# One gate and up tile moved from the attention's filler to the seven-product phase, in a block of sliding attention and a gated layer

## The chip, the core and the metric

The kernel runs on one NeuronCore of a Trainium2 chip, as one program. The metric is the device time of one execution in microseconds (us), given as the median of several runs.

The engines are called by the names of the profile: PE is TensorE's matmul, PEld its weight load, DVE is VectorE, ACT is ScalarE, POOL is GpSimd, and SP is SyncE, whose queue issues nearly all transfers here. L111 is line 111 of the kernel's file.

## The reference

Cut to what is computed (S = 2048 rows, D = 640 columns, 32 heads of 20, a window of 256 rows, a hidden width of 1728):

```python
xn = _layernorm(x)
q, k, v = (xn @ wqkv) split into 3 x 32 heads of 20
scores = q @ k.T * 20 ** -0.5        # only where 0 <= i - j < 256
o = softmax(scores) @ v
att = o.reshape(S, D) @ wo
h = gelu(xn @ w_gate) * (xn @ w_up)
out = x + att + h @ w_down
```

All tensors are float32.

## The kernel before

**Products.** A float32 factor is split in two parts, high and low, each of a type that TensorE takes at one pass. A plain product of two split factors is three products: high by high, low by high and high by low. With D = 640 in five slices of 128 rows, one group of 128 outputs by a chunk of 512 rows takes 3 x 5 = 15 TensorE products of 512 columns (`dense_steps`, L111). The 2048 rows are four chunks of 512.

**Stages.** The program has four stages on TensorE: the layer norm with the first projections; the attention; the phase of the gate and up products; and the phase of the last products (w_down and wo together, L1237).

**The attention.** It goes through 32 units, four chunks for each of eight groups of four heads. A unit has NS = 14 slots, and the code writes out by hand, slot by slot, what each engine gets to do. In a unit lie: the maxima (`max_pair`, L525 on PE and L529 on DVE, two pairs at slots 0, 4 and 8, and two more behind the output products), the scores with their exponential (`exp_piece`, L584 and L586, at slots 2, 4, 6, 8 and 10), the masks on POOL (`clear`, L597 and L600), and the output products of the unit before at slot 0 (`av_unit`, L624), whose sum POOL makes (L630). At slot 9 the k rows of a later unit are loaded and at slot 12 its q rows (`load_stack`, L496). The maxima of that later unit begin at slot 4 of the next unit. There are three q tiles, so a q load waits until the scores of the running unit have read the old one. The scores, maxima and output products use a ring of six PSUM banks; the filler has two banks of its own.

**The filler.** At the end of each slot TensorE gets products that have nothing to do with the unit, so that it has work while the other engines deal with the scores: `pull_fill(RATE / NS)`. A product of 512 columns counts 1.0 and one of 320 columns 0.65. Ahead of the first unit 12 portions of 8 and two of 8 are handed out. The generator `filler` gives them in this order: the last chunk of the first q and k tiles; then the list `sets`. A set ("qk", i) is the q tile i and the k tile i + 5, four chunks each, 120 products; a set ("gu", f) is the gate and the up tile f, four chunks each, 120 products too. At the place V1_AT the second half of V is projected (16 x 15 products of 320 columns); the first half's last rows come within the first set. The last set of the list, the half tile f = 13, is only split here and multiplied right behind the attention.

A projected q or k group goes on as follows (`save_qk`): ACT copies it to bf16 (L278), DVE subtracts (L274, into the single tile r), ACT copies again (L259), POOL subtracts (L260), and SP stores it to DRAM (L269), from where `load_stack` takes it. A gate and up group goes through ACT and DVE (L673 to L694) and is stored as h. Weights are loaded into the two buffers of `wrp` and split by ACT and POOL (L655, L660) while the set before runs; the split halves alternate between two pools, `pools[(s + 1) % 2]`.

**The phase of the gate and up products.** Tiles f = NFA to 12 are multiplied there by a scheme with seven products in place of eight (`gate_up_pair`, L970): for each tile and each of the two pairs of chunks, sums of the weights (`w_sums`) and of the rows (`x_sums`, made by POOL during the attention) take part, and there are 54 TensorE products of 512 columns, 108 for a tile, where the plain way has 120. A tile there has in addition its sums on DVE and its copies on ACT, and between them run jobs for the last phase (`work`).

```python
def pull_fill(n):
    debt[0] += n
    while debt[0] > 0:
        debt[0] -= next(fill, 1.0)
```

Of the kernel before, what the change touches and what calls it, by code (L numbers as in the profile page):

```python
# [25 lines left out]
NF = 14  # L26
# [5 lines left out]
NS = 14  # L32
BURSTS = 0, 4, 8
SCORES = {2: range(0, 3), 4: range(3, 5), 6: range(5, 7), 8: range(7, 9), 10: range(9, 12)}
RATE = 34.05
V1_AT = "gu", 0, 3
VEARLY = 2
VLEAD = 40
POOL_SLOTS = 13, 0, 1, 2, 3, 4, 5, 6, 7
MXD = 6  # L40
KSLOT = 9
LAG = 3, 5, 4, 4, 4, 4, 3, 3, 4, 3, 2, 1, 1, 1
NFA = 4
HD = D // 2
HR = 5
NQD = 9
# [25 lines left out]
def block_kernel(ctx, tc, x, wqk, wv, wgu, wdo, wdl, out):  # L72
# [414 lines left out]
    def load_stack(u, which=(0, 1)):  # L487
        g, c = divmod(u, NC)
        for m in range(80 * g // 128, (80 * g + 79) // 128 + 1):
            assert all((m + 5 * i, c) in done for i in which), (u, m)  # L490

        for i in which:
            dst, src, top, again = ((qs[u % NQ], qd[c], 1, 2), (ks[u % NK], kd[c], 0, 0))[i]
            for j in (0, 2):
                for p, part, n in ((j * 32, top, 2), (j * 32 + 2 * DH, again, 1), (64 - j * 32, 0, 3)):
                    nc.sync.dma_start(dst[p:p + DH * n, j:j + 2].rearrange("p j t -> p (j t)"),  # L496
                                      src[g, part:part + n].rearrange("s (d j) t -> (s d) (j t)",
                                                                      j=4)[:, j * C:(j + 2) * C])
# [140 lines left out]
    def load_gu(f):  # L639
        raws = []  # L640
        for i in range(2 if f < NF - 1 else 1):
            raw = wrp.tile([128, KT, 128], F32, name="wr", tag="wr")
            nc.sync.dma_start(raw, wgu[2 * f + i])
            raws.append(raw)
        return raws
# [4 lines left out]
    def split_later(pool, bufs, raw):  # L650
        hi = pool.tile([128, KT, 128], F32R, name="wqh", tag="wqh", bufs=bufs)
        lo = pool.tile([128, KT, 128], F32R, name="wql", tag="wql", bufs=bufs)

        def high():
            nc.scalar.activation(hi, raw, AF.Copy)  # L655
            for k in range(KT):
                defer(1 + k, when_free, low, k)

        def low(k):
            nc.gpsimd.tensor_tensor(out=lo[:, k], in0=raw[:, k], in1=hi[:, k].bitcast(F32), op=OP.subtract)  # L660

        defer(1, high)
        return hi, lo
# [37 lines left out]
                                   lambda k: xh[:, k, cs], lambda k: xl[:, k, cs], KT)  # L701
            defer(1, *((late, c4) if i else (c1,)))

    sets = [("qk", 1), ("qk", 2), ("qk", 3), ("gu", 0), ("qk", 4)]
    sets += [("gu", f) for f in range(1, NFA)] + [("gu", NF - 1)]
    pools = (wp, None), (hp, 2)
    rest = []

    def filler():
# [6 lines left out]
        for s, (kind, i) in enumerate(sets[:-1]):  # L716
            nxt = []
            after = sets[s + 1]
            for c in range(NC):
# [14 lines left out]
                if c in (1, 2) and c <= len(raws):  # L734
                    nxt.append(split_later(*pools[(s + 1) % 2], raws[c - 1]))
                if pending and (kind, i, c) == V1_AT:
                    pending = False
# [79 lines left out]
# [5 lines that stand above are left out]
    def attention():  # L822
# [18 lines left out]
        for u in range(NU + 1):  # L841
            for i in range(NS):
# [14 lines left out]
                if u + 3 < NU and i in (KSLOT, 12):  # L857
                    load_stack(u + 3, (int(i == KSLOT),))
                pull_fill(RATE / NS)
        while acts or idle:  # L860
# [458 lines left out]
    order.__enter__()  # L1319
    raws_w = load_gu(NFA)  # L1320
    banks = [psg.tile([128, C], F32, name="ps_g", tag=f"g{i}") for i in range(4)]
# [32 lines left out]

    raws_next = {NFA + 1: load_gu(NFA + 1)}
    for j, f in enumerate(range(NFA, NF - 1)):
        end = f + 1 == NF - 1
# [92 lines left out]
    for n, (p, k) in enumerate(steps):  # L1450
        i = n % (NQD + 1)
# [74 lines left out]
```

## Time and profile before

| | |
|---|---|
| median of 3 runs | 1032.83 us (1032.82, 1032.83, 1249.1) |
| the execution that was profiled | 1033.91 us |
| its span, first to last instruction | 1032.2 us |
| granted TensorE clock, mean | 0.999 |
| TensorE busy | 1020.8 us, 10941 products |
| moved from and to memory | 158.95 MB |

The page of a profile describes one execution. Its span is the time from the first to the last instruction; busy times are sums over an engine's instructions, and instructions on TensorE overlap, so the distance from one start to the next is what a product costs there. A row of the timeline gives the start, the length, the engine, the line and the tiles (written <- read), and in brackets the idle time of the engine ahead of it with what ended it. In the timeline and in the list of windows all times are counted from the span's start.

### The profile page before, as it was taken

The numbers are of one execution on the slowest core, as the hardware profiler recorded it, in microseconds if no ns is written. First come the engines' busy times: TensorE is split into PE (matmuls) and PEld (weight loads), VectorE is DVE, ScalarE is ACT, GpSimd is POOL, SyncE is SP. The second block draws the span as 40 slices with busy tenths as digits, with TensorE's granted clock in tenths as the row PEclk, the third lists the DMA queues.
The fourth block names the chain that finished last, engine by engine and source line by source line (L and its number), as shares of the span: only waits on it lengthen the run. The fifth ranks groups of instructions, "written<-read, shape, count | busy, mean of one in ns | idle before, by whom it ended". The sixth has DMA issues, their size and how long they took to land.

```text
span 1032.2 us, 28689 instructions
## 1 busy us (share of the span) xinstructions
PE 1020.8 (99%) x10941; PEld 853.4 (83%) x10941; DVE 710.5 (69%) x2007; ACT 528.3 (51%) x1120; POOL 380.0 (37%) x543
## 2 busy tenths in 40 slices
PE   8999999999999999999999999999999999999998
PEld 8987676777788877777777888888888999999998
DVE  8844655666665566676644778776556879888887
ACT  4444667766676666766666423222224544333332
POOL 5232777877665578667664111110110000000000
PEclk9999999999999999999999999999999999999999
DMA  5642464655432364534324557767127864434342
GB/s 203 191 143 70 136 198 138 179 160 178 123 106 86 96 177 135 158 121 133 121 67 134 178 200 244 249 230 245 67 79 259 263 215 146 138 124 131 111 133 93
DMA packets 105203, 158.95 MB, mean 154 GB/s; under 512 B 15420, under 2 KB 60092, under 8 KB 105064
## 3 DMA queue, kind: packets, MB, share of 16 engines
q1 hardware_dynamic: 102680, 150.95, 46.0%
q10 hardware_dynamic: 2384, 6.16, 1.9%
q8 instruction: 86, 1.41, 0.6%
q14 instruction: 53, 0.43, 0.1%
HBM read 101.78 MB, written 54.92 MB: 152 GB/s over the span
## 4 chain that ended last, share of the span: by engine, by line
PE 85%; DMA 4%; DVE 4%; POOL 2%; ACT 1%; issue 1%; SPq 1%; DVEq 0%; ACTq 0%; POOLq 0%
PE ps_g L970 20%; PE ps_d L111 20%; PE ps L1237 18%; PE ps_e L584 7%; PE ps_v L111 7%; PE ps_o L624 6%; PE ps_m L525 4%; PE ps_g L111 1%; DMA qs<-qd 1%; PE ps_t L182 1%; POOL pt L260 1%; DVE at L1075 1%; DMA kd<-pt 1%; DVE wb L1075 1%; DMA hd<-hr 1%
## 5 line engine op out<-in xcount | busy, mean ns | idle before, releaser
L529 DVE CUSTOM_DVE_ANT_0 junk<-ps_m,mask 128x288 bf16<-128x288 f32 (+2 forms) x512 | 197.6, 441 | 127.0 <-PE ps_m L525 126.1
L586 ACT ACTIVATE P<-ps_e 128x512 f32<-128x512 f32 (+2 forms) x384 | 195.4, 574 | 54.8 <-PE ps_e L584 53.6
L1237 PE MATMUL ps<-wb,at 128*128 128x320 f32 x999 | 156.4, 309 | 0.8 <-DVE xr L1263 0.8
L1237 PEld LDWEIGHTS ps<-wb,at 128*128 128x128 f32 x999 | 148.9, 188 | 1.6 <-issue 1.0
L597 POOL TENSOR_SCALAR_AFFINE_SELECT P<-P 128x512 f32<-128x512 f32 x128 | 84.5, 661 | 86.2 <-ACT P L586 80.6
L584 PE MATMUL ps_e<-qs,ks 124*128 124x128 bf16 (+2 forms) x704 | 107.2, 277 | 1.6 <-DVE mx L529 1.3
L111 PE MATMUL ps_d<-xh,wqh 128*128 128x512 f32 x350 | 105.2, 410 | 0.0
L111 PE MATMUL ps_d<-xh,wql 128*128 128x512 f32 x350 | 105.1, 410 | 0.0
L111 PE MATMUL ps_d<-xl,wqh 128*128 128x512 f32 x350 | 105.1, 409 | 0.0
L1237 PE MATMUL ps<-wt,at 128*128 128x320 f32 x552 | 89.3, 309 | 0.4 <-DVE u L1075 0.4
L584 PEld LDWEIGHTS <-ks 124*128 124x128 bf16 x704 | 51.6, 98 | 40.7 <-issue 24.2
L1237 PEld LDWEIGHTS ps<-wt,at 128*128 128x128 f32 x552 | 82.9, 188 | 0.9 <-DVE u L1075 0.9
L1191 ACT ACTIVATE at<-ss 128x512 fp32r<-128x512 f32 x59 | 37.3, 632 | 89.9 <-DVE ss L1075 89.9
L104 POOL TENSOR_TENSOR wql<-wr,wqh 128x640 fp32r<-128x640 f32 x11 | 17.7, 1609 | 173.1 <-PE ps_g L970 129.3
L600 POOL TENSOR_SCALAR_AFFINE_SELECT P<-P 128x512 f32<-128x512 f32 x112 | 72.0, 653 | 16.5 <-ACT P L586 16.4
L624 PE MATMUL ps_o<-P,v 64*32 64x320 f32 (+5 forms) x2816 | 77.1, 347 | 0.2 <-POOL P L600 0.2
L111 PEld LDWEIGHTS ps_d<-xh,wql 128*128 128x128 f32 x350 | 63.9, 189 | 13.0 <-issue 2.1
L111 PEld LDWEIGHTS ps_d<-xh,wqh 128*128 128x128 f32 x350 | 63.2, 189 | 13.2 <-issue 2.6
L111 PEld LDWEIGHTS ps_d<-xl,wqh 128*128 128x128 f32 x350 | 63.6, 189 | 12.5 <-issue 2.3
L624 PEld LDWEIGHTS ps_o<-P,v 64*32 64x32 f32 x2816 | 66.9, 106 | 4.8 <-POOL P L600 1.4
L260 POOL TENSOR_TENSOR pt<-r,pt 128x512 bf16<-128x512 f32 x40 | 46.9, 1173 | 56.6 <-ACT pt L259 56.3
L525 PE MATMUL ps_m<-ks,qs 60*32 60x96 bf16 (+4 forms) x3008 | 61.0, 244 | 1.8 <-DMA qs<-qd 1.4
(196 smaller groups left out, 1906.9 us busy)
## 6 DMA issues: line engine op xcount, KB each, us to landing
hr<-hd SPq DMA_DIRECT2D x104, 128.0 KB
hd<-he SPq DMA_DIRECT2D x50, 256.0 KB
wr<-wgu SPq DMA_DIRECT2D x27, 320.0 KB
qs<-qd SPq DMA_DIRECT2D x64, 120.0 KB
ks<-kd SPq DMA_DIRECT2D x64, 120.0 KB
xi<-x SPq DMA_DIRECT2D x16, 320.0 KB
qs<-qd SPq DMA_DIRECT2D x64, 80.0 KB
ks<-kd SPq DMA_DIRECT2D x64, 80.0 KB
```

The lines of the kernel that those rows point to most:

```text
L111: nc.tensor.matmul(ps, a(k), b(k), start=n == 0, stop=n == 3 * nk - 1)
L260: nc.gpsimd.tensor_tensor(out=pt[:, l, :], in0=r, in1=pt[:, 1, :], op=OP.subtract)
L525: nc.tensor.matmul(ps[32 * h:32 * h + 32, lo:hi], q[rows, j, q0:q0 + 32], keys, start=True, stop=True, tile_position=(64 * r, 32 * h))
L529: nc.vector.tensor_tensor_reduce(out=junk[:, 0:n], in0=ps[:, 0:n], in1=mask[:, 288 - n:288], scale=1.0, scalar=NEG, op0=OP.add, op1=OP.max ...
L584: nc.tensor.matmul(ps[:, col:col + n], k[0:QROWS, j, kc:kc + 128], q[0:QROWS, j, q0:q0 + n], start=True, stop=True)
L586: nc.scalar.activation(pt[:, j, lo:hi], ps[:, lo:hi], AF.Exp, scale=SCALE)
L597: nc.gpsimd.affine_select(out=a, in_=a, pattern=[[0, 4], [1, 128]], compare_op=OP.is_ge, fill=0.0, base=0, channel_multiplier=-1)
L600: nc.gpsimd.affine_select(out=a, in_=a, pattern=[[0, 4], [-1, 128]], compare_op=OP.is_ge, fill=0.0, base=-1, channel_multiplier=1)
L624: nc.tensor.matmul(halves[h][32 * j:32 * j + 32, q0:q0 + n], v[rows, w0_:w0_ + 32], pts[u, bi][rows, j, col:col + n], start=i == 0, stop=i ...
L970: nc.tensor.matmul(ps, i, j, start=first and n == 0, stop=n == len(work) - 1, skip_group_check=True)
L1191: nc.scalar.activation(hi[:, 3:7], s, AF.Copy)
L1237: nc.tensor.matmul(ps[bank][:, 0:HD], *work[bank][j], start=bank not in begun, stop=final[p, bank] == n and j == len(work[bank]) - 1, skip ...
```

## The change

Tile f = 3 leaves the filler and is multiplied in the phase behind the attention, which then has the tiles 3 to 12. The four q and k sets follow each other without the tile f = 0 between the third and the fourth. V's second half, which stood behind tile 0, now stands within the last q and k set, behind its chunk 1. The rate of the filler goes from 34.05 to 30.4 per unit.

```diff
-RATE = 34.05
-V1_AT = "gu", 0, 3
+RATE = 30.4
+V1_AT = "qk", 4, 1
...
-NFA = 4
+NFA = 3
...
-    sets = [("qk", 1), ("qk", 2), ("qk", 3), ("gu", 0), ("qk", 4)]
-    sets += [("gu", f) for f in range(1, NFA)] + [("gu", NF - 1)]
+    sets = [("qk", i) for i in range(1, 5)] + [("gu", f) for f in range(NFA)] + [("gu", NF - 1)]
```

Three places in the order of the instructions show what moves. (One line fewer stands ahead of the attention's end in the new file, so its later lines are one lower.)

The first is SP's queue in the fourth unit of the attention, around the q load of chunk 2 for the second group of heads (qs is the q tile, ks the k tile; qd and kd are the stored q and k rows in DRAM, pt the tile they are stored from, wr and wvr raw weights). Before:

```order
L496 DMA ks_171<-kd_90 60x1024
L269 DMA qd_84<-pt 64x3x512 x2
L238 DMA wr<-wqk 128x640 x2
L496 DMA qs_166<-qd_86 40x1024
L496 DMA qs_166<-qd_86 20x1024
```

Now:

```order
L496 DMA ks_171<-kd_90 60x1024
L295 DMA wvr<-wv 128x320 x2
L496 DMA qs_166<-qd_86 40x1024
L496 DMA qs_166<-qd_86 20x1024
L496 DMA qs_166<-qd_86 60x1024
L496 DMA qs_166<-qd_86 40x1024
L496 DMA qs_166<-qd_86 20x1024
L496 DMA qs_166<-qd_86 60x1024
L269 DMA qd_84<-pt 64x3x512 x2
L238 DMA wr<-wqk 128x640 x2
```

The store of the projected q rows and the two weight loads have moved from ahead of the q load to behind it; V's raw weights stand ahead of it now. In the units behind this one the new queue repeats itself: q load, q store, the stores of the unit's output, k store, k load.

The second place is on TensorE, the end of the last unit: the last scores (ps_e), the filler (ps_d) and the beginning of the last output products (ps_o). Before:

```order
L584 MATMUL ps_e<-qs_167,ks_172 128x384
L111 MATMUL ps_d<-xh_79,wqh 128x512 x2
L111 MATMUL ps_d<-xh_79,wql 128x512 x5
L111 MATMUL ps_d<-xl_83,wqh 128x512 x3
L624 MATMUL ps_o<-P,v 32x320 x8
```

Now:

```order
L584 MATMUL ps_e<-qs_167,ks_172 128x384
L111 MATMUL ps_d<-xh_79,wql 128x512 x3
L111 MATMUL ps_d<-xl_83,wqh 128x512 x5
L624 MATMUL ps_o<-P,v 32x320 x8
```

Ten filler products stand between the last scores and the last output products before, eight now. Behind the output products came two more of the filler before; now the filler is used up there and the half tile 13 (ps_g) follows at once.

The third is on ScalarE, where V's second half begins (L332 saves a V group, L673 and L683 belong to a gate and up group, L278 and L259 to a q or k group). Before:

```order
L673 ACTIVATE gs<-ps_d 128x512
L674 ACTIVATE he<-ps_d 128x512
L628 ACTIVATE ob<-ps_o 128x512
L629 ACTIVATE P<-ps_o 128x512
L586 ACTIVATE P<-ps_e 128x512 x5
L683 ACTIVATE he<-he 128x512
```

Now:

```order
L278 ACTIVATE pt<-ps_d 128x512
L655 ACTIVATE wqh<-wr 128x640
L586 ACTIVATE P<-ps_e 128x512 x5
L259 ACTIVATE pt<-r 128x512
L332 ACTIVATE v<-ps_v 128x4x20 x4
```

The last group ahead of V was a gate and up group of tile 0 and is now a k group of the fourth set.

## The prediction, made before the changed kernel ran

> **What bounds the kernel now.** I read the page's busy times first, then the attention and the phases behind it as stretches, then the chain that ended last, TensorE's waits, and at last single stretches of the timeline.
>
> ```profile
> span 1032.2 us, 28689 instructions
> PE 1020.8 (99%) x10941; PEld 853.4 (83%) x10941; DVE 710.5 (69%) x2007; ACT 528.3 (51%) x1120; POOL 380.0 (37%) x543
> ...
> core 0: us, PE busy (x) PEld busy (x) DVE busy (x) ACT busy (x) POOL busy (x), PEclk, DMA share, GB/s
> 104.80:552.10 447.30, 443.93 (x7307) 331.97 (x7308) 271.61 (x1075) 302.14 (x655) 314.14 (x461) 1.00 0.46 136
> 555.30:568.90 13.60, 13.60 (x61) 11.22 (x61) 11.63 (x17) 8.31 (x13) 2.72 (x2) 1.00 0.58 176
> 568.90:788.90 220.00, 220.00 (x973) 182.13 (x972) 155.09 (x259) 69.93 (x131) 23.90 (x16) 1.00 0.55 189
> ...
> 104.80:162.50 57.70, 56.53 (x907) 41.08 (x908) 34.64 (x141) 40.50 (x82) 41.72 (x60) 1.00 0.53 157
> 162.50:220.50 58.00, 56.04 (x945) 40.12 (x944) 36.09 (x145) 39.63 (x81) 50.39 (x73) 1.00 0.57 167
> 220.50:281.70 61.20, 61.07 (x1011) 44.55 (x1014) 37.97 (x149) 41.33 (x84) 43.03 (x64) 1.00 0.50 154
> ```
>
> The span is 1032.2 us; the execution that was profiled took 1033.91 us, so 1.7 us lie around the span, and the median of the runs shown is 1032.83 us. TensorE is busy 99%. The first long stretch runs from the first unit's output products to the last unit's, 31 units of attention: 447.30/31 = 14.43 us a unit, with 447.30 - 443.93 = 3.37 us of TensorE idle. Of these, 1.17 and 1.96 us lie in the first eight units (the two rows from 104.80 and 162.50). The seven-product phase (568.90 to 788.90) has no idle at all. The granted clock is 1.00 everywhere. So what is to be priced is TensorE's instructions, and then the few places where it waits.
>
> ```profile
> 555.28 13.64 PE ps_g L111 x60
> 568.92 208.09 PE ps_g L970 x918
> ...
> L970 PE MATMUL ps_g<-xh,wqh x162: 389/389/389, 568.8 to 788.4; 128*128 128x512 f32 x162
> ```
>
> The chain gives the price: 60 plain products of 512 columns follow each other in 13.64 us, 0.2273 us each, and 918 of the seven-product phase in 208.09 us, 0.2267 us each. (The 389 ns of the last row is the length of one instruction; they overlap, and only the distance counts.) A tile of the phase has 54 such products for each of its two pairs of chunks, 108, of which 18 are of the row's kind: 162/18 = 9 tiles, f = 4 to 12.
>
> **The change part by part.** (1) Tile f = 3 leaves the filler: 2 weights x 4 chunks x 15 = 120 products, 120 x 0.2273 = 27.28 us of TensorE less in the attention. RATE goes along: it hands out 30.4 instead of 34.05 products in each of 32 units, 3.65 x 32 = 117 less. (2) The tile joins the phase: 108 x 0.2267 = 24.48 us more, as TensorE there never waits and the phase has done nine such tiles at this pace. The tile brings 23 VectorE, 14 ScalarE and 2 GpSimd instructions; those of the nine tiles keep these engines busy 155.09, 69.93 and 23.90 of 220 us and hide under the products. If that cover were gone, VectorE's share, 155/9 = 17 us, would show; at 70% busy it isn't. The sum of both is -2.80 us.
>
> (3) Every filler segment gets shorter, by 3.65/14 = 0.26 product or 0.059 us a slot. What waits under the filler gets less cover: mainly the load of the next q tile on SP's queue, which may begin when the last scores (slot 10) have read the old tile and must have landed at the maxima of slot 4 of the next unit. Eight filler segments lie between, so the cover shrinks by 8 x 0.059 = 0.47 us.
>
> ```profile
> 145.04 1.33 SPq L269 DMA_DIRECT2D qd<-pt  x2
> 146.41 1.12 SPq L238 DMA_DIRECT2D wr<-wqk  x2
> 147.63 2.28 SPq L496 DMA_DIRECT2D qs<-qd  x6
> 153.90 0.19 PE L525 MATMUL ps_m<-ks,qs 60*32 60x32 bf16 x1 [0.49 <-DMA qs<-qd]
> 154.74 0.52 PE L525 MATMUL ps_m<-ks,qs 60*32 60x32 bf16 x31 [0.65 <-DMA qs<-qd]
> ...
> 179.74 3.36 SPq L496 DMA_DIRECT2D qs<-qd  x6
> 185.00 0.38 PE L525 MATMUL ps_m<-ks,qs 60*32 60x32 bf16 x28
> ...
> 307.24 2.15 SPq L496 DMA_DIRECT2D qs<-qd  x6
> 315.74 0.46 PE L525 MATMUL ps_m<-ks,qs 60*32 60x32 bf16 x32
> ```
>
> The profile has no landing times, but three loads bound them. At 185.00 the maxima start without a wait 1.90 us behind the end of the issue (179.74 + 3.36), so a load can land in 1.90 us. At 307 there are 6.35 us, far more than needed; this is the stage of V's products. At 153.90 and 154.74 TensorE waits, 3.99 and 4.83 us behind the issue's end: the issue was late because a store of projected q rows and two weight loads stood ahead of it (145.04 to 147.53), and the transfers were crowded. So the cost of (3) lies between nothing (1.90 us suffices) and 0.47 us in each unit that also projects q and k. In the new order of SP's queue 15 q loads have a q store behind them, which marks these units: 15 x 0.47 = 7.1 us.
>
> The Trainium skill, page "DMA: Bandwidth & Descriptors", section "Anatomy of one DMA — SWDGE (gpsimd) path", gives about 2.0 us as the fixed part of one transfer on GpSimd's path. By that figure (an estimate, as these loads go by SP's queue) a q load would fit everywhere but where it is issued late, and (3) would cost nothing; the first of the loads above agrees, the one at 147.63 took twice that.
>
> (4) The order of the sets and the new rate change what stands ahead of those loads. Each unit now gives out 30.4 products, that is one q and one k product group of 15 each, so one store of each kind per unit, always at the same slots; before it was 34.05/15 = 2.27, drifting through the unit. The new queue of SP shows it: the q store stands behind the q load in each of these units, and none stands ahead. What that may save is bounded by the idle of the attention: 0 to 3.37 us. The second wait of that stage has the same root:
>
> ```profile
> 173.37 1.17 POOL L260 TENSOR_TENSOR pt<-r,pt 128x512 bf16<-128x512 f32 x1
> 174.57 0.69 DVE L274 TENSOR_TENSOR r<-ps_d,pt 128x512 f32<-128x512 f32 x1 [4.09 <-POOL pt L260]
> 175.69 1.13 PE L584 MATMUL ps_e<-qs,ks 124*128 124x128 bf16 x6 [1.34 <-DVE mx L529]
> ```
>
> Two groups were projected so close together that VectorE stood 4.09 us for the single tile r until GpSimd had done with the one before, the maxima behind it came late, and TensorE waited 1.34 us for a bank. With 2.03 groups a unit instead of 2.27 this comes less often. Of the 2.48 us in these two places I take 1.2 as saved, and 0.8 as lost by (3), where the rows lean to its lower end (1.90 us is enough): -0.4 us together.
>
> (5) V's second half: a product of 512 columns counts 1 in the filler, one of 320 columns 0.65. Ahead of it stood 30 (chunk 3 of the first pair) + 58.5 (the rest of V's first half) + 3 x 120 (q and k sets) + 120 (tile 0) = 568.5, of which 12 x 8 + 16 = 112 are handed out before the first unit: it begins 456.5/34.05 = 13.4 units into the attention. Now it is 30 + 58.5 + 360 + 60 = 508.5, and (508.5 - 112)/30.4 = 13.0 units; its 16 x 15 x 0.65 = 156 end at 18.0 and 18.2. The last rows are needed by unit 19, whose output products stand at the head of unit 20: 1.8 units, some 25 us, to spare. Cost nothing.
>
> (6) The end of the attention: 8 filler products instead of 10 stand between the last scores and the last output products, and the 2 behind them are gone.
>
> ```profile
> 551.32 0.84 PE L111 MATMUL ps_d<-xl,wqh 128*128 128x512 f32 x3
> 552.09 2.54 PE L624 MATMUL ps_o<-P,v 64*32 64x320 f32 x96
> 552.71 0.64 POOL L597 TENSOR_SCALAR_AFFINE_SELECT P<-P 128x512 f32<-128x512 f32 x1
> ```
>
> The last mask ends at 553.35; the products that read it are the last third of the 2.54 us, from 553.8. They come 2 x 0.227 = 0.45 us earlier, just the slack; 0 to 0.2 us, taken as nothing.
>
> Sum: 24.48 - 27.28 - 0.4 = -3.2 us. The profiled execution would go from 1033.91 to 1030.7 us, and the median from 1032.83 to **1029.6 us**.
>
> **The rivals.** *The loads decide* (slower): in the new beat the store of k rows stands straight ahead of the k load, and the q load behind that, in each unit. If GpSimd is late with its part of the k rows, all three are late each time, and TensorE waits at slot 4. It decides from the point where a load's cover, 1.90 us at the tightest, is gone; its price is (3)'s upper end, 7.1 - 2.8 = +4.3 us, 1037.1 us. For it: GpSimd's 50.39 of 58.00 us in the stretch from 162.50. Against it: fewer groups per unit, so less for GpSimd.
>
> *All idle of the attention goes* with the regular beat: -2.8 - 3.37, 1026.7 us. For it, 3.13 of the 3.37 us lie where groups were projected; against it, less cover.
>
> *The attention does not shrink*, as something else paces it: the 27.28 us turn into waits and the phase still costs 24.48: 1057.3 us. Against it: 0.8% idle of TensorE, and GpSimd, the busiest of the others, would have about 50 us for four units of 54.7 us (58.0 - 4 x 0.83). The Trainium skill, "Perfetto Trace Analysis", section "Identifying the Most-Contended Engine", says that matmul busy time is no good measure and weight-load busy is better: 331.97 of 447.30 us here is 74%, against 83% in the phase. By that rule the attention has room on TensorE and this case could be true; the waits that the trace shows there speak against it.
>
> *The change doesn't do what it says*, the tenth tile costing as much as it saves (120 products): 0 instead of -2.8, 1032.4 us with the -0.4. Against it: the count of products in the code.
>
> **How the numbers follow.** The forecast has 0.60 (1028.3 to 1031.5), the loads 0.18 (1031.5 to 1037.1), all idle gone 0.16 (1026.7 to 1028.3), no shrinking 0.03, nothing gained 0.03. The range from 1026.7 to 1037.1 takes in the bounds of (3) and (4) and leaves out only the case of no shrinking. A measurement of this kernel can tell 2%, some 20 us, from no change; only the case of no shrinking passes that, so slower has 0.03, faster 0.01 and same 0.96.
>
> **What would show it.** The chain should hold 108 more products of the phase and the phase should be 244.5 us long; a unit of attention should last (14.43 - 0.83) = 13.6 us, the first output products of the last unit coming some 26 us earlier. TensorE's idle between the first and the last unit's output products should be 2 to 4 us. I am wrong if that idle is above 6 us, if the phase has waits, or if a unit stays above 14 us.

## The result: 1048.68 us, 1.4% slower, and the profile after

The changed kernel takes 1048.68 us (median of 5 runs, 1046.04 to 1049.54) against 1032.83 us before, a ratio of 1.014 with a 95% interval of 1.0128 to 1.0152. The ratio comes from the single runs, without the one of 1249.1 us before, which lies far above all others; the two medians by themselves give 1.0153. The execution that was profiled took 1048.68 us, 14.8 more than the one of before. The forecast was 1029.6 us, at most 1037.1. By the 2% of the prediction this is still "same", to which it gave 0.96, but the interval is narrow enough to tell 1.4% from nothing.

The first lines of the page after, and the two rows of its chain that stand for the half tile 13 and the seven-product phase (start, length, engine, tile, line, count):

```profile
span 1047.0 us, 28712 instructions
...
PE 1023.6 (98%) x10929; PEld 851.1 (81%) x10929; DVE 717.2 (69%) x2018; ACT 524.6 (50%) x1120; POOL 373.2 (36%) x535
```

```profile
545.75 13.82 PE ps_g L111 x60
559.57 244.80 PE ps_g L969 x1080
```

TensorE has 12 products fewer than before, as counted, and is busy 2.8 us longer in a span that is 14.8 us longer. The phase is as forecast: ten tiles in one unbroken piece of 244.80 us. So the time is lost ahead of it. The output products of the attention mark its length (line 624: shortest, median and longest duration in ns, then the first and the last start). Before:

```profile
L624 PE MATMUL ps_o<-P,v x2816: 214/376/504, 103.7 to 554.4; 64*32 64x320 f32 x67, 64*32 64x64 f32 x32, 64*32 64x256 f32 x29, 64*32 64x128 f32 x29
```

After:

```profile
L624 PE MATMUL ps_o<-P,v x2816: 214/376/504, 102.9 to 545.5; 64*32 64x320 f32 x67, 64*32 64x64 f32 x35, 64*32 64x192 f32 x30, 64*32 64x256 f32 x26
```

450.7 us have become 442.6, 8.1 less, where 26 were forecast; the phase begins at 559.57 instead of 568.92, 9.35 earlier, while 27.28 us of work are gone. Some 18 us are lost in the attention. Where, the list of stretches shows (columns as in the prediction). The first stretch, 104 to 300 us, holds most of the q and k groups, before also tile 0; it is the q and k stage. The second, 300 to 520, holds V's second half (289 to 355 us after), the last q and k groups (to 388 us after, to 415 before) and the gate and up tiles. Before:

```profile
104.00:300.00 196.00, 192.59 (x3225) 140.88 (x3209) 122.57 (x492) 132.30 (x273) 149.21 (x224) 1.00 0.52 155
300.00:520.00 220.00, 219.89 (x3703) 167.36 (x3701) 138.48 (x554) 146.89 (x338) 146.26 (x212) 1.00 0.43 127
```

After:

```profile
104.00:200.00 96.00, 89.27 (x1507) 63.52 (x1507) 56.57 (x230) 62.70 (x127) 73.67 (x107) 0.98 0.50 143
200.00:300.00 100.00, 95.16 (x1663) 70.74 (x1663) 60.97 (x252) 65.94 (x147) 76.98 (x118) 1.00 0.57 167
...
104.00:300.00 196.00, 184.43 (x3169) 134.26 (x3170) 117.54 (x481) 128.64 (x273) 150.65 (x224) 0.99 0.53 156
300.00:520.00 220.00, 217.39 (x3795) 161.51 (x3801) 138.50 (x567) 144.62 (x332) 140.94 (x209) 1.00 0.40 120
...
390.00:520.00 130.00, 127.78 (x2219) 90.61 (x2226) 86.61 (x341) 82.85 (x167) 84.20 (x127) 1.00 0.42 127
```

TensorE's idle goes from 3.41 to 11.57 us in the first stretch and from 0.11 to 2.61 us in the second, 10.7 us more together; of the 2.61 us, 2.22 lie behind 390 us, where only gate and up tiles are left (the last row). This part is the gate and up stage; where an expectation below gives a number for that stage, it means the whole second stretch. A clock of 0.98 in the first 96 us adds some 0.02 x 96 = 1.9 us. The remainder of the 18, some 5 us, is in no row. A part of it can hide in the stops themselves: a product of 512 columns has a length of 0.389 us, while the next could start after 0.227, so up to 0.16 us of a stop behind it counts as busy. I have not counted this stop by stop, and it is not shown.

What TensorE waits for in the whole run after (total us, times, longest):

```profile
PE ps_m L525 <- DMA qs<-qd: 8.1, 8, 1.6
...
PE ps_e L584 <- DVE mx L529: 1.3, 8, 0.2
PE ps_o L624 <- POOL P L600: 1.3, 1, 1.3
```

The first of these was 1.4 us, 3 times, before. The same list for SP's queue between 104 and 300 us has the stores' wait for GpSimd's part of a projected group, after:

```profile
SPq L269 <- POOL pt L260: 32.9, 11, 4.8
```

And before:

```profile
SPq L269 <- POOL pt L260: 18.9, 8, 3.7
```

How the one makes the other is seen in a unit of this stage, here from 203 us on (timeline of SP's queue, of GpSimd and of TensorE after):

```profile
205.56 1.26 SPq L269 DMA_DIRECT2D kd<-pt  x2
206.88 0.60 SPq L295 DMA_DIRECT2D wvr<-wv  x1
207.59 3.49 SPq L496 DMA_DIRECT2D ks<-kd  x6
211.18 0.35 SPq L760 DMA_DIRECT2D td<-tx  x1
211.64 2.17 SPq L496 DMA_DIRECT2D qs<-qd  x6
...
203.18 1.22 POOL L600 TENSOR_SCALAR_AFFINE_SELECT P<-P 128x512 f32<-128x512 f32 x2
204.37 1.16 POOL L260 TENSOR_TENSOR pt<-r,pt 128x512 bf16<-128x512 f32 x1
...
215.19 0.17 PE L525 MATMUL ps_m<-ks,qs 60*32 60x32 bf16 x1 [0.19 <-issue]
216.16 0.45 PE L525 MATMUL ps_m<-ks,qs 60*32 60x32 bf16 x31 [0.81 <-DMA qs<-qd]
```

GpSimd gets to the k group (L260) only behind its masks (L600) and ends at 205.53. The store of that group is at the head of SP's queue, and starts at 205.56. The k load, which has nothing to do with this store, is issued behind it, the q load behind that; its issue ends at 213.81, and at 216.16, 2.35 us later, TensorE has waited 0.81 us. This order, k store, k load, q load, comes back in each of the 13 units that fall into this stage. Their q loads start 2.1 to 5.3 us behind the end of the last scores that read the old tile, and in eight of the 13 TensorE then waits for them.

In the gate and up stage there is no q or k group. There the waits are for VectorE, mostly for its maxima, where the end of a gate and up group (L687, L694) follows the end of a unit's maxima (VectorE's timeline after, then TensorE's):

```profile
437.45 0.72 DVE L538 TENSOR_SCALAR nm<-mx 128x16 bf16<-128x16 f32 x1
438.20 0.66 DVE L539 SCALAR_TENSOR_TENSOR nm<-mx,nm 128x16 bf16<-128x16 f32 x1
438.78 0.68 DVE L687 TENSOR_TENSOR gs<-ps_d,gs 128x512 f32<-128x512 f32 x1
439.56 0.69 DVE L694 SCALAR_TENSOR_TENSOR he<-he,gs 128x512 f32<-128x512 f32 x1
...
440.68 0.22 PE L546 MATMUL ps_n<-identb,nm 128*128 128x128 bf16 x1 [0.30 <-DVE mx L529]
```

VectorE gets to the next maxima (L529) only at 440.17, behind these four, and TensorE stands until 440.68. That the four are the cause is read from the rows.

The theory: **the place of the beat decides**. 30.4 products in a unit are two groups of 15, so whatever a group does on ACT, DVE, POOL and SP comes at nearly the same slots in each unit (the 0.4 left over moves it only slowly); at the place where it lies now it is in the way, each time. The rivals: the order of the sets, the load slots, or GpSimd's load as such. That SP's queue is the path from the place to the loss, and not something else that GpSimd does late, is a question of its own, which the later experiments take up.

### The profile page after: what moved, and what is told of

It is laid out like the page before. It is cut to its first block, busy times and chain, and to the rows that moved or that the text cites. A ratio compares the mean times of both kernels' runs of the same rounds, so it can differ in the third digit from the quotient of the medians.

```text
span 1047.0 us, 28712 instructions
## 1 busy us (share of the span) xinstructions
PE 1023.6 (98%) x10929; PEld 851.1 (81%) x10929; DVE 717.2 (69%) x2018; ACT 524.6 (50%) x1120; POOL 373.2 (36%) x535
## 4 chain that ended last, share of the span: by engine, by line
PE 64%; DVE 4%; DMA 2%; issue 1%; POOL 1%; ACT 1%; SPq 0%; DVEq 0%; POOLq 0%
PE ps_g L969 23%; PE ps L1236 19%; PE ps_d L111 6%; PE ps_e L584 4%; PE ps_o L624 4%; PE ps_v L111 3%; PE ps_m L525 2%; PE ps_g L111 1%; DMA hr<-hd 1%; DVE junk L529 1%; DMA stg<-wtd 1%; DVE nm L538 0%; ACT P L586 0%; DVE ss L1074 0%; DVE at L1074 0%
## 5 line engine op out<-in xcount | busy, mean ns | idle before, releaser
L529 DVE CUSTOM_DVE_ANT_0 junk<-ps_m,mask 128x288 bf16<-128x288 f32 (+2 forms) x512 | 197.7, 442 | 156.4 <-PE ps_m L525 155.6
L597 POOL TENSOR_SCALAR_AFFINE_SELECT P<-P 128x512 f32<-128x512 f32 x128 | 84.1, 659 | 86.2 <-ACT P L586 79.6
L111 PE MATMUL ps_d<-xh,wqh 128*128 128x512 f32 x310 | 98.2, 420 | 0.0
L111 PE MATMUL ps_d<-xl,wqh 128*128 128x512 f32 x310 | 95.1, 412 | 0.0
L111 PE MATMUL ps_d<-xh,wql 128*128 128x512 f32 x310 | 91.3, 408 | 0.0
L600 POOL TENSOR_SCALAR_AFFINE_SELECT P<-P 128x512 f32<-128x512 f32 x112 | 70.3, 638 | 13.7 <-ACT P L586 13.7
L111 PEld LDWEIGHTS ps_d<-xl,wqh 128*128 128x128 f32 x310 | 55.9, 190 | 14.6 <-issue 5.8
L525 PEld LDWEIGHTS <-qs 60*32 60x32 bf16 x3008 | 32.8, 90 | 42.8 <-issue 30.1
L260 POOL TENSOR_TENSOR pt<-r,pt 128x512 bf16<-128x512 f32 x40 | 46.9, 1172 | 53.3 <-ACT pt L259 53.3
L111 PEld LDWEIGHTS ps_d<-xh,wql 128*128 128x128 f32 x310 | 56.6, 189 | 10.6 <-issue 0.5
```

Of the source, the lines that this page charges most:

```text
L111: nc.tensor.matmul(ps, a(k), b(k), start=n == 0, stop=n == 3 * nk - 1)
L260: nc.gpsimd.tensor_tensor(out=pt[:, l, :], in0=r, in1=pt[:, 1, :], op=OP.subtract)
L525: nc.tensor.matmul(ps[32 * h:32 * h + 32, lo:hi], q[rows, j, q0:q0 + 32], keys, start=True, stop=True, tile_position=(64 * r, 32 * h))
L529: nc.vector.tensor_tensor_reduce(out=junk[:, 0:n], in0=ps[:, 0:n], in1=mask[:, 288 - n:288], scale=1.0, scalar=NEG, op0=OP.add, op1=OP.max ...
L597: nc.gpsimd.affine_select(out=a, in_=a, pattern=[[0, 4], [1, 128]], compare_op=OP.is_ge, fill=0.0, base=0, channel_multiplier=-1)
L600: nc.gpsimd.affine_select(out=a, in_=a, pattern=[[0, 4], [-1, 128]], compare_op=OP.is_ge, fill=0.0, base=-1, channel_multiplier=1)
```

## The experiments

Each time is the median; the time of the kernel before, measured alongside, stands beside it. Two experiments first split the change: the new order of the sets with the old count of tiles and the old rate, and the old order with the new ones.

**The order alone.** The kernel before with

```
-V1_AT = "gu", 0, 3
+V1_AT = "qk", 4, 2
...
+    sets = [("qk", i) for i in range(1, 5)] + [("gu", f) for f in range(NFA)] + [("gu", NF - 1)]
```

> The kernel before, with the new order of the sets alone (four q and k sets in a row, V's second half within the fourth, behind chunk 2); four tiles in the filler and the rate 34.05 as before. Theory A, the beat: waits come from the rate, which at 30.4 gives one q and one k group per unit at fixed slots, so that a late store of k rows stands ahead of every load; at 34.05 the groups drift. Then 1031 to 1035 us and 3 to 6 us of idle of TensorE in the attention. Theory B, the order: waits come from q and k sets that follow each other without a pause; then 1040 us or more, with waits for q loads in the units 4 to 17.

Measured: 1033.15 us, before 1032.66; ratio 0.9995 (0.9982 to 1.0008). At the old rate the order costs nothing.

**The rate alone.** The changed kernel with the sets as before (tile 0 between the third and the fourth q and k set) and V1_AT = "gu", 0, 2; the rate 30.4 and NFA = 3 stay.

> The changed kernel with the old order of the sets (tile 0 between the third and the fourth q and k set, V's second half behind its chunk 2); three tiles in the filler and the rate 30.4 as changed. Theory A, the beat: 1043 to 1050 us, the waits for q loads up to about 170 us as in the changed kernel, and those behind about 350 us too. Theory B, the order: 1029 to 1034 us.

Measured: 1045.17 us, before 1032.66; ratio 1.0123 (1.0098 to 1.0148). The loss comes with the rate of 30.4 and the three tiles, which go together, not with the order.

**The store later.** If the store's wait holds SP's queue, issue it when its data is there:

```
-            defer(2, store)
+            defer(7, store)
```

> The changed kernel with the stores of projected q and k rows issued seven slots behind the last GpSimd step in place of two, so that in each unit they stand behind both loads in SP's queue. If the queue's order makes the q loads late, TensorE's waits for them (8 to 12 us in the changed kernel's trace between 100 and 300 us) go, and the time is 1037 to 1041 us. If the load on GpSimd or the transfers themselves make them late, it stays at 1046 to 1050 us.

Measured: 1049.87 us, before 1032.66; ratio 1.0165 (1.0135 to 1.0195). No gain; the time lies where the rival was expected. Yet the waits for q loads are gone from TensorE's list, but ACT now waits for the tile pt (three buffers) that the late store holds, and TensorE for ACT (ACT's waits in this run, then TensorE's):

```profile
ACT pt L278 <- DMA kd<-pt: 10.0, 8, 2.2
```

```profile
PE ps_m L525 <- ACT P L586: 4.0, 5, 1.7
```

So the queue's order does make the q loads late: with the store behind them they are on time. But one wait was traded for another, and this run didn't tell how much of the lost time comes by the queue.

**The maxima later.**

```
-MXD = 6
+MXD = 7
```

> The changed kernel with the product that turns the maxima (max_end) one slot later, 7 in place of 6. If the waits of 0.4 to 1.2 us per unit behind 350 us come from that product, which stands in TensorE's queue ahead of maxima that VectorE has not finished, they go: 4 to 6 us less, 1042 to 1045 us. If VectorE is late as such, the wait only moves to the next scores, and the time stays within 1.5 us of 1048.7.

Measured: 1045.46 us (1043.94 to 1052.31), before 1032.66; ratio 1.013 (1.0094 to 1.0166). By its interval this is not told apart from the changed kernel. Its trace, of the slowest of these runs, has TensorE busy 218.84 of the 220 us of the second stretch (217.39 after), and 181.41 of 196 in the first (184.43 after).

**The beat moved.** GAP is the portion of the filler ahead of the first unit; less of it puts every later group later in its unit, by 8 products or 3.7 slots. The products stay the same; the eight that are not handed out there come at the filler's end.

```
-GAP = 16
+GAP = 8
```

> The changed kernel with 8 in place of 16 filler products ahead of the first unit, so that the beat of one q and one k group per unit comes some four slots later: k stores at slots 12 and 11 in place of 9 and 8, q stores at 5 to 1 in place of 0. Theory A1, the place of the beat: the time depends on where the groups fall; here the k load stands ahead of the k store, the q load still behind it: some of the waits go, 1038 to 1046 us. Theory A2, less cover: every slot has 0.06 us less filler, wherever the groups fall: 1046 to 1050 us with about the same idle of TensorE.

Measured: 1031.81 us, before 1033.34; ratio 0.9992 (0.9976 to 1.0008). All of the loss is gone, more than either theory expected. Its two stretches:

```profile
104.00:300.00 196.00, 192.53 (x3346) 140.79 (x3345) 120.82 (x502) 137.19 (x294) 156.61 (x233) 1.00 0.57 162
300.00:520.00 220.00, 219.24 (x3753) 163.64 (x3751) 141.19 (x553) 150.76 (x336) 147.68 (x214) 1.00 0.40 119
```

Its output products, and its phase in the chain:

```profile
L624 PE MATMUL ps_o<-P,v x2816: 214/376/505, 100.9 to 528.0; 64*32 64x320 f32 x66, 64*32 64x64 f32 x32, 64*32 64x192 f32 x29, 64*32 64x128 f32 x29
```

```profile
543.66 244.85 PE ps_g L969 x1080
```

TensorE's wait for q tiles, and SP's for GpSimd between 104 and 300 us:

```profile
PE ps_m L525 <- DMA qs<-qd: 3.4, 5, 1.0
```

```profile
SPq L269 <- POOL pt L260: 12.3, 14, 1.6
```

And the k load, the k store and the q load in the timeline of SP's queue, at the place shown of after:

```profile
209.53 2.23 SPq L496 DMA_DIRECT2D ks<-kd  x6
...
212.76 1.31 SPq L269 DMA_DIRECT2D kd<-pt  x3
214.17 3.03 SPq L496 DMA_DIRECT2D qs<-qd  x6
```

The k load now stands ahead of the k store, and SP waits less for the store: 12.3 us in place of 32.9. The first stretch is as full as before the change (192.53 and 192.59 us), the second nearly so. The last output products start 554.4 - 528.0 = 26.4 us earlier than before, as the forecast had it (some 26), and the phase begins 568.92 - 543.66 = 25.3 us earlier.

The other direction, about 3 slots earlier:

```
-GAP = 16
+GAP = 22
```

> The changed kernel with 22 filler products ahead of the first unit, so that the beat comes some three slots earlier: k stores at slots 5 and 2, well ahead of the k load at 9, q stores at 12 and 11, ahead of the q load. Theory A1, the place of the beat: another time than with 16 or 8, by 4 us or more, either way. Theory A2, less cover: 1046 to 1050 us again.

Measured: 1034.71 us, before 1033.34; ratio 1.002 (1.0005 to 1.0034), with TensorE busy 192.94 of 196 and 220.00 of 220 us. It is 14 us from the time at 16, as theory A1 asks, but only 3 from that at 8. So it isn't "later is better", but the place at 16 that is bad.

**The k load a slot earlier.**

```
-KSLOT = 9
+KSLOT = 8
```

> The changed kernel with the k load emitted at slot 8 in place of 9. In the units 1 to 5 it then stands ahead of the k store (slot 9), in later units (k store at slot 8) still behind. If the k store in front makes the loads late, TensorE's waits for q loads go in the trace up to about 180 us and stay behind that: 3 to 5 us less, 1043 to 1046 us. If not, 1047 to 1050 us.

Measured: 1042.88 us, before 1033.34; ratio 1.0098 (1.0083 to 1.0113). A part of the loss is gone, and the run has its own control. In the early units the k load now precedes the store (SP's queue from 140 us on), in the later ones, whose store moves up as well, it doesn't (from 200 us on):

```profile
140.84 4.24 SPq L496 DMA_DIRECT2D ks<-kd  x6
145.18 1.33 SPq L269 DMA_DIRECT2D kd<-pt  x3
...
147.57 2.19 SPq L496 DMA_DIRECT2D qs<-qd  x6
...
200.45 1.25 SPq L269 DMA_DIRECT2D kd<-pt  x2
201.82 2.69 SPq L496 DMA_DIRECT2D ks<-kd  x6
...
205.53 3.36 SPq L496 DMA_DIRECT2D qs<-qd  x6
```

From the end of a q load's issue to its first maxima there are 2.5 to 3.4 us in units 5 to 8 (0.8 to 2.6 after), and 0.3 to 1.1 us, no better than after, in units 9 to 11. TensorE's waits for q tiles go accordingly: up to 181 us from 4.4 us after to none here, behind that only from 3.7 to 2.9.

**GpSimd freed in the q and k stage.** The sums for the phase (`x_sums`) move out of it:

```
-XS0, XSN = 24, 50
+XS0, XSN = 196, 28
...
-                at(XS0 + XSN * i + 5 * j, when_free, fn)
+                at(XS0 + XSN * i + 27 * j // 10, when_free, fn)
```

> The changed kernel with the 80 sums of the rows on GpSimd (x_sums) moved out of the stage of the q and k groups: from slots 24 to 419 to slots 196 to 416, in closer steps. GpSimd then has about 2 us less per unit of 14 us up to slot 190. If GpSimd's lateness with the k rows is what makes the loads late, the waits between 100 and 290 us go from 13.9 us in the changed kernel to below 6 and the time to 1037 to 1041 us, unless the later stage pays. If GpSimd is not the cause, they stay above 10 us.

Measured: 1043.7 us, before 1033.34; ratio 1.0104 (1.0088 to 1.0119). GpSimd is busy 19.5 us less than after between 104 and 300 us, yet two thirds of the loss stay; the idle between 104 and 300 us, 6.6 us, lies between what the two theories expected. Its stretches:

```profile
104.00:200.00 96.00, 89.97 (x1547) 64.21 (x1548) 55.00 (x238) 63.77 (x129) 62.78 (x92) 1.00 0.50 144
200.00:300.00 100.00, 99.41 (x1711) 74.04 (x1709) 60.74 (x261) 70.03 (x162) 68.36 (x105) 1.00 0.52 153
300.00:520.00 220.00, 216.17 (x3752) 159.15 (x3750) 141.14 (x561) 142.89 (x321) 164.06 (x240) 1.00 0.43 127
```

Behind 200 us it helps as much as it can, ahead of it hardly at all (89.97 against 89.27), though GpSimd has 10.9 us less to do there; and the stage that has the sums now is slower for it. GpSimd's load has a share in the loss; it isn't the whole of it. SP's wait for L260 between 104 and 300 us is even longer here than after, 36.3 us against 32.9, while TensorE's for q tiles falls from 8.1 to 4.3 us: how long SP stands doesn't say what it costs.

**Is there a better place?** GAP = 6, GAP = 10, and GAP = 8 together with MXD = 7:

> Changed kernel with GAP 16 -> 6, the beat one or two slots later than with GAP 8. If the place of the beat decides and there is a broad good stretch around GAP 8, 1030 to 1033 us; if GAP 8 was a narrow lucky place, 1036 us or more. Best case by the base sum (24.48 - 27.28 against the kernel before's 1033): about 1030.

> Changed kernel with GAP 16 -> 10, the beat between GAP 8 (1031.8) and GAP 16 (1048.7). If the place of the beat decides by the margin of the loads, between the two but nearer to GAP 8, 1032 to 1040 us; a smooth fall of the loss with the distance from GAP 16. If the two runs differ for another reason, no order in it.

> Changed kernel with GAP 16 -> 8 and MXD 6 -> 7. MXD 7 took some 2 us of the waits for the maxima in the gate and up stage at GAP 16; at GAP 8 that stage has almost no waits left (219.24 of 220 us busy), so by the theory of the beat it gains nothing here: 1031 to 1033 us. If MXD 7 were a gain of its own, 1029 to 1030.

Measured, beside 1033.27 us before: 1035.94 us (ratio 1.0027, 1.0015 to 1.0039) at 6, 1033.02 us (1.0005, 0.9996 to 1.0015) at 10, and 1040.53 us (1.0078, 1.0061 to 1.0095) at 8 with MXD = 7. So 8 and 10 lie in one good stretch, which ends toward 6; the time at 6 lies between the two that were expected. The last one was a miss: with the turned maxima a slot later the q loads are late again, 6.4 us of TensorE's waits in 7 against 3.4 in 5, and the first stretch has TensorE busy 188.35 of 196 us. SP's wait for L260 is as short there as at GAP = 8 (11.6 and 12.3 us); the loads wait for the store of the turned maxima into the q tile instead (12.4 us against 8.8). So the k store isn't the only thing that can make them late. None of the versions beats the kernel before beyond the intervals; GAP = 8 is the best of them.

**The store on another queue.** The direct test: the place stays bad (GAP = 16), but the k stores are issued by GpSimd itself, behind its own L260, so that SP's queue has nothing to wait for ahead of the loads.

```
-                nc.sync.dma_start(dst[g, :, b:b + n, :].rearrange("p m t -> m p t"), pt[p - n:p])
+                (nc.sync if t < 5 else nc.gpsimd).dma_start(dst[g, :, b:b + n, :].rearrange("p m t -> m p t"), pt[p - n:p])
```

> Changed kernel, GAP 16 as it is, but the stores of the projected k rows (L269, about 2 in a unit) are issued by GpSimd itself, behind its own L260, instead of by SP, so SP's queue cannot stand still for them; the k and q loads keep their slots and their queue. If the k store at the head of SP's queue is what makes the q loads late (32.9 us of SP's waits for L260 between 104 and 300 us, 8.1 us of TensorE's for q tiles): those waits nearly vanish and the q and k stage goes from 184.43 of 196 us busy to about 192; the gate and up stage keeps its loss, so 1037 to 1042 us. If GpSimd's lateness acts in another way (tiles r and pt, masks, output sums), or its own issuing of the stores costs as much as it frees, 1046 us or more.

Measured: 1042.42 us, before 1032.31; ratio 1.0088 (1.0075 to 1.0102). Its two stretches:

```profile
104.00:300.00 196.00, 191.05 (x3252) 134.22 (x3253) 122.92 (x497) 133.59 (x289) 172.53 (x262) 1.00 0.54 159
300.00:520.00 220.00, 216.95 (x3764) 160.59 (x3763) 139.73 (x562) 144.21 (x327) 143.55 (x213) 1.00 0.40 119
```

TensorE's longest wait between 104 and 300 us, then SP's longest there:

```profile
PE ps_o L624 <- POOL P L600: 3.3, 5, 1.5
```

```profile
SPq L269 <- POOL pt L260: 29.5, 11, 4.3
```

The k stores on GpSimd in that stretch (count, shortest, median and longest issue in ns):

```profile
L269 POOL DMA_DIRECT2D kd<-pt x33: 516/630/677, 115.8 to 287.2; - x33
```

Not one wait for a q tile is left, and the first stretch is busy 191.05 us instead of 184.43. The q loads of the 13 units now start from 0.4 us ahead of the end of the last scores to 1.1 us behind it, where they had started 2.1 to 5.3 us behind. Most of the 4.95 us of idle that remain are waits for GpSimd's masks (L600), and it has 33 issues of 0.63 us more to do. The second stretch keeps its loss (216.95), 1.84 us of it behind 390 us, where there are no such stores. That SP's waits would go too was wrong: it still waits 29.5 us, now for the q stores, which stand behind the q load. The same wait, at a place where nothing urgent stands behind it, costs TensorE nothing.

## Why the prediction was wrong, by its own steps

- **(1) and (2), the moved tile: right.** The phase has 1080 products in 244.80 us, 0.2267 us each as before and without a wait, and the 108 of the tenth tile are the forecast 24.5 us. The attention can shrink by nearly the work taken out of it: at GAP = 8 the phase begins 25.3 of the 27.28 us earlier. Of the -2.80 us even that place shows only 1.5 (1033.34 to 1031.81), inside its interval.
- **(4), the regular beat: this step failed.** I bounded it as a gain, 0 to 3.37 us, because a drifting beat showed two clashes in the trace and a regular one would "come less often". A beat in step with the unit repeats whatever its place brings, and only the place decides: the same 30.4 products a unit give 1035.9 us at GAP 6, 1031.8 at 8, 1033.0 at 10, 1034.7 at 22, and 1048.7 at 16. In place of the -1.2 us this step cost some 17 us (1048.68 - 1031.81). The term was bounded by the idle of the kernel before, which bounds a gain and says nothing of a loss.
- **(3), less cover for the loads: the size failed.** I counted the shorter filler, 0.47 us a unit, from a load that was on time with 1.90 us. After, 2.35 us were not enough in the unit shown; one time that sufficed is no bound for the others. The cover shrank not by the filler but by the store ahead of the load, which my own order of SP's queue showed.
- **The rival "the loads decide"** named the mechanism, and the place at which it acts, but priced it by (3), at most 7.1 us; against it stood "fewer groups per unit, so less for GpSimd". GpSimd has as much to do between 104 and 300 us as before (150.65 and 149.21 us). When it gets to the group counts, not how many there are. The store on another queue shows the loads' share: 6.3 us of the changed kernel's time, with what the new issues cost already taken off. Of the rest, a part is seen at the masks and a part in the gate and up stage.
- **(6)** was right: after, the last third of the last output products waits 0.20 us for the last mask (at 545.30 us, for L597), the upper end of "0 to 0.2 us". From the last output product to the phase lie 559.57 - 545.5 = 14.1 us after and 568.92 - 554.4 = 14.5 before, less the two filler products that stood behind. For **(5)**, no wait for V's rows stands in TensorE's list.
- "The attention does not shrink" was wrong as a rule: at GAP = 8 the weight loads are busy 140.79 of 196 us, no more than before, and the attention shrank all the same. The page of the Trainium skill that was weighed there, "Perfetto Trace Analysis", section "Identifying the Most-Contended Engine", would read the 134.26 us after as more room on TensorE; here they are mostly the trace of waits behind a queue.
- Of the signs that I had named, two came true: idle above 6 us and, with (545.5 - 102.9)/31 = 14.3 us, a unit above 14.

What stays open is the share of each wait in the gate and up stage: that the place of the beat decides there too is shown (217.39 of 220 us busy in the second stretch at GAP 16, 219.24 at 8, 220.00 at 22), that it acts by VectorE is read from the rows and wasn't tried by itself.

## What to carry to other kernels

Where background work is handed out at a rate that fits its period to that of the loop, price it at its place: write down for one period which queue entry stands behind which wait, and take the loss once per iteration. A queue that issues in its order, as SP's did here, turns one late store into late loads, so ask of each wait who stands behind it, not how long it is. And before a change of rate is dropped or kept, move its phase: one constant was worth 17 us here.

## What the runs showed of the hardware

A store's issue takes GpSimd 0.63 us in the median (0.52 to 0.68), while SP's issues of the like q stores in the same run took 0.44.

The profile doesn't give the landing of SP's loads, but where TensorE waited for a q tile, the end of the wait bounds it. In five units after (with waits that end at 139, 155, 170, 201 and 216 us) it came 1.7 to 2.6 us behind the end of the load's issue, so the 1.90 us from which the prediction worked lie toward the low end.

The granted clock fell once in the attention, behind two of the longest waits. TensorE's timeline after, and the list of stretches:

```profile
168.76 0.17 PE L525 MATMUL ps_m<-ks,qs 60*32 60x32 bf16 x1 [0.71 <-DVE nm L539]
170.58 0.45 PE L525 MATMUL ps_m<-ks,qs 60*32 60x32 bf16 x31 [1.65 <-DMA qs<-qd]
```

```profile
170.00:175.00 5.00, 4.42 (x48) 3.07 (x48) 1.60 (x8) 2.81 (x6) 2.66 (x5) 0.69 0.62 174
```

Two waits of 0.71 and 1.65 us nearly next to each other, and the clock of the next 5 us is 0.69, which costs 0.31 x 5 = 1.6 us more. In stretches of 1 us it is 1.00 up to 171, 0.96 from 171 to 172 and 0.50 from 172 to 175 us. The Trainium skill, "TensorE: Matmul & The Clock Gate", section "What's actually happening", says that the clock is halved after an idle window of about 3.4 us; the half agrees, and here 2.36 us of idle, with 0.17 us of work between, were enough. I had priced waits by their own length; here two of them cost two thirds of it again in clock.
